# A dense layer by Strassen on pairs of token tiles, with the layer norm folded into its neighbours

## Chip, cores and metric

One NeuronCore of a Trainium2 chip runs the whole program. The metric is the device time of one execution in microseconds; lower is better. Times are medians of several executions; a profile is one execution.

## What is computed

Three stages follow each other on 2304 tokens of width 512. First, attention in chunks of 64 tokens. Second, a mixture of 8 experts, each with a hidden layer of 1024, weighted by eight rounds of row and column scaling. Third, the stage that the change touches (cut from the reference):

```
h = x @ w_in                                   # 2304x512 @ 512x1024
e = exp(h - max(h)); sm = e / (sum(e) + 1e-9)
solu = h * sm
ln = (solu - mean(solu)) / sqrt(var(solu) + 1e-6) * g_ln
return ln @ w_out                              # 2304x1024 @ 1024x512
```

w_in and w_out arrive as 64-bit floats and are turned into 32-bit ones on the chip.

## The kernel before

The program is unrolled, and every engine runs its instructions in the order in which they are written. Each 32-bit operand of a matmul is a pair of parts: `split` (L149) makes the high part on ScalarE (ACT) and the rest by a subtraction on VectorE (DVE) or GpSimd (POOL). A product takes three passes over these parts (PASSES3, L41).

**The experts.** They run as 96 units (3 passes over tokens, 32 weight blocks each) in the loop at L1203. One unit has seven slots; in each, `l1` (L738) issues one Strassen product of the first expert layer (six matmuls of 384 columns, L653) and `l2s` (L833) one half of a product of the second layer of two units earlier (six matmuls, L847). Weights come from DRAM by `w_load` (L617) on the SP queue. DVE adds the banks of `l1` and accumulates `l2s` into `acc`; POOL makes the sums and low parts of the hidden layer for `l2s` (`h_less` L679, `h_put` L665).

**Preparation of w_in and w_out.** From unit 35 on, one step of a list `prep` runs in slots 1, 3 and 5 of each unit (L1255). There are 16 chunks of 128x512, eight of each matrix, with ten steps each: a load (L907), seven steps of bit work on DVE (`mlp_steps`, L912), w_out rows scaled by g_ln on ACT (L949), `parts` (a split with POOL) and two stores of the parts (L957).

**The seam.** In unit 95 the parts of w_in are loaded (`load_in`, eight loads of 512 KB, tag `six`). Then 14 halves of `l2s` remain, numbered k = 0 to 13. They take PSUM banks from a ring of four (tag `r`) and each waits for DVE to have emptied the bank of four halves before. After k = 7, `mlp_b(0)` is issued; after k = 13 the loads of w_out's parts (`load_out`) and the tail begin.

**The tail.** For each of 18 token tiles: `mlp_a` splits x (ACT, DVE); `mlp_b` issues 24 matmuls of 512 columns into two PSUM banks (L1005), then the row maximum on DVE (L1019) and the exponential on ACT (L1020); `mlp_n` multiplies (L1025), takes statistics (L1026 to L1037, one power on POOL) and normalises on DVE (L1038); `mlp_c` transposes 128x1024 on TensorE (PE) in eight steps (L1050) and splits the result (ACT, DVE); `mlp_d` issues 24 matmuls (L1062), an eviction on ACT (L1072) and the store. The loop at L1296 issues b(s), c(s-1), n(s), d(s-2). The seven last sums of the experts' result (`l2s_sums`, L870) run on DVE between tiles 2 and 9, one for each tile.

Of the kernel before, what the change touches and what calls it, by code (L numbers as in the profile page):

```python
# [9 lines left out]
F32 = mybir.dt.float32  # L10
F32R = mybir.dt.float32r
# [33 lines left out]
def chunk_attention_sinkhorn_moe_solu_kernel(  # L45
# [74 lines left out]
    def six(shape, dt, name):  # L120
        return work.tile(shape, dt, tag="six", bufs=15, name=name)
# [7 lines left out]
    def two(shape, dt, name):  # L129
        return work.tile(shape, dt, tag="two", bufs=14, name=name)  # L130
# [762 lines left out]

    kept = {}
    for i in range(2):
        for s_ in range(2):
            kept[i, s_] = dram.tile([P, 4096], F32, name=f"kept{i}_{s_}")

    raw64 = {}

    def load_mlp(n):
        i, j = divmod(n, 8)
        src, r0, c0 = (w_in, (j // 2) * P, (j % 2) * 512) if i == 0 else (w_out, j * P, 0)
        raw64[n] = four([P, 512, 2], U32, f"wd{n}")
        nc.sync.dma_start(  # L907
            out=raw64[n].rearrange("p f w -> p (f w)"),
            in_=src.bitcast(U32)[r0:r0 + P, 2 * c0:2 * c0 + 1024],
        )  # L910

    def mlp_steps(n):  # L912
        i, j = divmod(n, 8)
        s = {}
        ts, stt = nc.vector.tensor_scalar, nc.vector.scalar_tensor_tensor


        def one():
            s["lo"], s["hi"] = raw64[n][:, :, 0], raw64[n][:, :, 1]
            s["b"] = two([P, 512], U32, f"wb{n}")  # L920
# [30 lines left out]
        def parts():  # L951
            s["p"] = [two([P, 512], F32R, f"wp{n}_{s_}") for s_ in range(2)]
            split(*s["p"], s["b"].bitcast(F32), nc.gpsimd)

        def store():
            for s_ in range(2):
                nc.sync.dma_start(  # L957
                    out=kept[i, s_][:, j * 512:(j + 1) * 512], in_=s["p"][s_].bitcast(F32)
                )

        return [one, two_, three, round_, rounded, size, flush_, parts, store]

    m_in, m_out = {}, {}

    def load_in(kk, s_):
        t = six([P, F], F32R, f"mi{kk}_{s_}")
        nc.sync.dma_start(out=t.bitcast(F32), in_=kept[0, s_][:, kk * F:(kk + 1) * F])
        m_in[kk, s_] = t

    def load_out(n0, n1):  # L970
        for n in range(n0, n1):
            f, s_ = divmod(n, 2)
            if n % 3 == 0:
                m_out["t"] = six([P, 3, DM], F32R, f"mo{n}")
            t = m_out["t"]
            nc.sync.dma_start(
                out=t[:, n % 3].bitcast(F32), in_=kept[1, s_][:, f * DM:(f + 1) * DM]
            )
            m_out[f, s_] = t[:, n % 3]

# [10 lines left out]
        )  # L991
        xa[t] = x

    def mlp_a(t):
        x = xa.pop(t)
        xm[t] = [wtile([P, KD, P], F32R, f"xm{t}_{i}") for i in range(2)]
        split(xm[t][0], xm[t][1], x)

    def mlp_b(t):
        x = xm.pop(t)  # L1000
        ph = bank2(f"mh{t}")
        for n in range(2):
            for kk in range(KD):
                for i, (a, c) in enumerate(PASSES3):
                    nc.tensor.matmul(  # L1005
                        ph[:, n * 512:(n + 1) * 512],
                        x[a][:, kk, :],
                        m_in[kk, c][:, n * 512:(n + 1) * 512],
                        start=(kk == 0 and i == 0),
                        stop=(kk == KD - 1 and i == 2),  # L1010
                    )
# [6 lines left out]
        r2 = small.tile([P, 1], F32, tag="r2", name=f"r2{t}")  # L1018
        nc.vector.tensor_reduce(out=nm, in_=ph, axis=AX.X, op=ALU.max, negate=True)  # L1019
        nc.scalar.activation(out=ex, in_=ph, func=AF.Exp, bias=nm, scale=1.0, accum_out=su)  # L1020
        stage[t] = (ph, ex, un, su, st, mv, r2)

    def mlp_n(t):
        ph, ex, un, su, st, mv, r2 = stage.pop(t)
        nc.vector.tensor_tensor(out=un, in0=ph, in1=ex, op=ALU.mult)  # L1025
# [12 lines left out]
        nc.vector.tensor_scalar(  # L1038
            out=un, in0=un, scalar1=mv[:, 0:1], scalar2=r2, op0=ALU.subtract, op1=ALU.mult
        )  # L1040
        ln[t] = un

    def mlp_c(t):
        un = ln.pop(t)
# [11 lines left out]
    def mlp_d(t, f0=0, f1=KF):  # L1056
# [12 lines left out]
        if f1 < KF:  # L1069
            return  # L1070
        ob = two([P, DM], F32, f"ob{t}")
        nc.scalar.activation(out=ob, in_=po.pop(t), func=AF.Copy)  # L1072
        nc.sync.dma_start(out=out[t * P:(t + 1) * P, :], in_=ob)


    with tc.manual_schedule():
# [91 lines left out]
        def x_steps(p, eng):  # L1168
# [34 lines left out]
        for n in range(NM):  # L1203
# [30 lines left out]
            if n == NM - 1:  # L1234
                for t in range(3):
                    mlp_x(t)
            apart = n < 4
            parts = [(j, d, i) for d in (0, 2) for j in range(2) for i in range(2)]
            for i in range(7):
# [7 lines left out]
                    elif i < 5:  # L1247
                        x_load(p + 1, XOPS[2 + i], nc.scalar)
                if n == NM - 1:
                    load_in(*divmod(i, 2))  # L1250
                if n != NU - 1 or i > 2:
                    run_w(2 if i < 4 or n == 0 else 1)
                if n:
                    run_side(1)
                if n > NU + 2 and i in (1, 3, 5) and prep:  # L1255
                    prep.popleft()()
                if NU > n > NQ and i in ((1, 2, 4, 6) if n in PLAIN else (2,)) and late:
                    late.popleft()()
# [82 lines left out]
```

## Time and profile before

| | us |
|---|---|
| median of 3 runs (1759.47 to 1763.54) | 1759.66 |
| the profiled execution | 1766.55 |
| its span, first to last instruction | 1764.7 |
| PE, DVE, ACT, POOL busy in the span | 1740.2, 1365.3, 626.6, 1093.5 |
| seam, first half of `l2s` after unit 95 | starts at 1530.64 |

Times in rows are microseconds from the start of the span, durations of one instruction in a group are in nanoseconds where a row says mean or gives min/median/max. PE counts as busy when a matmul is in its pipeline; ends of matmuls are modelled, so the distance between starts is the safer measure.

### The profile page before, as it was taken

How to read it: one execution, taken by the hardware profiler on the slowest of the kernel's cores; microseconds unless marked ns; L12 is line 12 of the kernel's file. 1: busy time of each engine (PE TensorE's matmuls, PEld its weight loads, DVE VectorE, ACT ScalarE, POOL GpSimd, SP SyncE). 2: the span in 40 equal slices, each digit the busy share in tenths (PEclk: the TensorE clock that was granted, in tenths of full speed). 3: DMA queues.
4: the chain of work that ended last, by engine and by line, in shares of the span. 5: the costliest groups of instructions: out<-in, count | busy, mean ns of one | idle time of the engine just before them, and what ended most of it. 6: DMA issues, size and time to landing. Idle time of an engine off the chain costs nothing. (4 is left out here: it accounts for less than half of the span.)

```text
span 1764.7 us, 32057 instructions
## 1 busy us (share of the span) xinstructions
PE 1740.2 (99%) x10809; PEld 1685.7 (96%) x10809; DVE 1365.3 (77%) x2249; ACT 626.6 (36%) x1424; POOL 1093.5 (62%) x1203
## 2 busy tenths in 40 slices
PE   8999999999999999999999999999999999999999
PEld 7899999999999999999999999999999999988887
DVE  6768888888987778787777688878787877776664
ACT  6743444444444233333332222232322222222222
POOL 2877988888887277778777756666656565400000
PEclk9999999999999999999999999999999999999999
DMA  9677899899899999989989999888888888931210
GB/s 220 181 247 257 296 325 335 311 343 326 319 324 330 348 331 339 336 297 351 310 296 340 341 328 369 301 284 283 282 263 276 281 275 255 314 108 45 66 49 30
DMA packets 299203, 481.45 MB, mean 273 GB/s; under 512 B 47248, under 2 KB 99616, under 8 KB 299040
## 3 DMA queue, kind: packets, MB, share of 16 engines
q1 hardware_dynamic: 298320, 475.47, 79.1%
q10 hardware_dynamic: 720, 3.93, 0.5%
q8 instruction: 87, 1.43, 0.3%
q14 instruction: 76, 0.62, 0.1%
HBM read 332.94 MB, written 146.35 MB: 272 GB/s over the span
## 5 line engine op out<-in xcount | busy, mean ns | idle before, releaser
L673 POOL TENSOR_TENSOR ho_T<-hT,ho_T 128x384 fp32r<-128x384 f32 x252 | 275.3, 1094 | 195.8 <-ACT ho_T L672 179.3
L796 PE MATMUL y<-h,w_A 128*128 128x384 f32 x1536 | 303.8, 335 | 0.5 <-DVE acc L823 0.5
L796 PEld LDWEIGHTS y<-h,w_A 128*128 128x128 f32 x1536 | 269.2, 188 | 1.3 <-ACT w_S L599 1.1
L672 ACT ACTIVATE ho_B<-hp 128x384 fp32r<-128x384 f32 x192 | 101.0, 526 | 418.6 <-DVE hp L706 410.4
L847 PE MATMUL y<-ho_T,wl_S 128*128 128x384 f32 x1152 | 231.4, 336 | 2.0 <-DMA wl_S<-wk 1.9
L152 POOL TENSOR_TENSOR w_A<-raw,w_A 128x256 fp32r<-128x256 f32 x224 | 173.2, 786 | 81.9 <-ACT w_A L151 77.5
L867 DVE TENSOR_TENSOR acc<-y,acc 128x768 f32<-128x768 f32 (+1 forms) x217 | 199.9, 923 | 24.5 <-PE y L847 24.3
L751 DVE TENSOR_TENSOR t<-Y,s 128x384 f32<-128x384 f32 x192 | 106.2, 553 | 136.5 <-PE Y L653 94.2
L847 PEld LDWEIGHTS y<-ho_T,wl_S 128*128 128x128 f32 x1152 | 203.1, 188 | 3.4 <-issue 2.2
L681 POOL TENSOR_TENSOR hT<-hp,hp 128x384 f32<-128x384 f32 x126 | 133.2, 1079 | 99.7 <-DVE hp L706 89.8
L672 ACT ACTIVATE ho_T<-hT 128x384 fp32r<-128x384 f32 x256 | 131.6, 516 | 124.6 <-POOL hT L681 119.9
L653 PE MATMUL Y<-x_T,wl_S 128*128 128x384 f32 x768 | 154.1, 335 | 0.4 <-DVE t L751 0.3
L653 PE MATMUL X<-x_B,wl_A 128*128 128x384 f32 x768 | 154.3, 335 | 0.0
L847 PE MATMUL y<-ho_B,wl_A 128*128 128x384 f32 x768 | 153.7, 334 | 0.5 <-DVE acc L867 0.4
L673 DVE TENSOR_TENSOR ho_B<-hp,ho_B 128x384 fp32r<-128x384 f32 x192 | 145.7, 759 | 3.9 <-ACT ho_B L672 3.3
L681 POOL TENSOR_TENSOR hT<-hp,hT 128x384 f32<-128x384 f32 x126 | 143.8, 1142 | 0.0
L1036 POOL TENSOR_TENSOR r<-r,mhalf 128x1 f32<-128x1 f32 x18 | 9.9, 550 | 208.5 <-DVE r L1033 208.5
L847 PEld LDWEIGHTS y<-ho_B,wl_A 128*128 128x128 f32 x768 | 134.7, 188 | 1.6 <-DVE acc L867 0.7
L653 PEld LDWEIGHTS Y<-x_T,wl_S 128*128 128x128 f32 x768 | 135.1, 188 | 1.1 <-DVE t L751 1.1
L653 PEld LDWEIGHTS X<-x_B,wl_A 128*128 128x128 f32 x768 | 135.4, 188 | 0.0
L823 DVE TENSOR_TENSOR acc<-y,acc 128x768 f32<-128x768 f32 (+1 forms) x132 | 118.9, 901 | 5.3 <-PE y L796 4.1
L152 POOL TENSOR_TENSOR w_S<-ws,w_S 128x256 fp32r<-128x256 f32 x128 | 103.0, 823 | 6.1 <-ACT w_S L151 6.1
(169 smaller groups left out, 3452.9 us busy)
## 6 DMA issues: line engine op xcount, KB each, us to landing
wl_S<-wk SPq DMA_DIRECT2D x512, 256.0 KB, 4.9
wl_A<-wk SPq DMA_DIRECT2D x384, 256.0 KB, 4.7
wk<-w_S SPq DMA_DIRECT2D x256, 256.0 KB, 3.6
wk<-w_A SPq DMA_DIRECT2D x192, 256.0 KB, 3.4
raw<-in_moe_w_dram SPq DMA_DIRECT2D x71, 512.0 KB, 5.8
sh<-spread SPq DMA_DIRECT2D x64, 192.0 KB, 5.4
kept<-wp SPq DMA_DIRECT2D x32, 256.0 KB, 4.2
xk_T<-x_T SPq DMA_DIRECT2D x8, 768.0 KB, 4.3
```

Of the source, the lines that this page charges most:

```text
L152: (eng or nc.vector).tensor_tensor(out=lo, in0=src, in1=hi.bitcast(F32), op=ALU.subtract)
L653: nc.tensor.matmul(b, w[:, a, kk, :], x[:, c, kk, :], start=(first and kk == 0 and n == 0), stop=(kk == 1 and n == 2), skip_group_check=no ...
L672: nc.scalar.activation(out=hi, in_=x, func=AF.Copy)
L673: f = lambda: eng.tensor_tensor(out=lo, in0=x, in1=hi.bitcast(F32), op=ALU.subtract)
L681: eng.tensor_tensor(out=hb[m, n], in0=hb[m, a], in1=hb[m, b], op=ALU.subtract)
L751: nc.vector.tensor_tensor(out=c_of[n], in0=bank_, in1=c_of[other], op=ALU.add)
L796: nc.tensor.matmul(y, wo2[u, f"A{d // 2 + 1}{f + 1}"][:, a, i * P:(i + 1) * P], h[:, c, f, :], start=(f == 0 and n == 0), stop=(f == 1 and ...
L823: nc.vector.tensor_tensor(out=at, in0=y, in1=at, op=ALU.add)
L847: nc.tensor.matmul(y, wo2[unit(m + q_)[1], wn][:, a, i * P:(i + 1) * P], hop[m // 2, bn][:, q_, c, :], start=(q_ == 0 and o == 0), stop=(q ...
L867: nc.vector.tensor_tensor(out=at, in0=y, in1=at, op=ALU.add)
L1036: nc.gpsimd.tensor_tensor(out=r2, in0=r2, in1=mhalf, op=ALU.pow)
```

## The change

The first dense layer takes two token tiles at once (a pair r is tiles 2r and 2r+1) and replaces eight block products by seven of six matmuls each, with sums of x blocks on POOL before and five additions of PSUM banks on DVE after. The operands of w_in (B11, T1, B22, T3, T2, B21, T4) are formed once in `prep`. w_out, scaled by g_ln, is stored whole, its mean over the rows is taken by a matmul with a constant matrix and subtracted, and the parts are stored; so the tail needs no subtraction of the mean. The factor of the norm is applied in ACT's last eviction, and `un` is transposed as it is. `prep` now has 203 steps: 98 for w_in, 72 for w_out, 33 for the mean; when 64 are left it runs in slots 0 to 5 of each unit. `load_in` reads 28 blocks of 128x512 in 12 loads (the first three into tag `V`). The diff, cut to its core:

```
     def mlp_steps(n):
...
+        def put_g():
+            nc.sync.dma_start(out=kept_g[:, j * 512:(j + 1) * 512], in_=s["b"].bitcast(F32))
...
+        def less(to, a, b):
...
+            nc.gpsimd.tensor_tensor(op=ALU.subtract, **x)
...
+    def mean_steps():
+        def load(j, new):
+            s[j] = new([P, 512], F32, f"wg{j}")
+            nc.sync.dma_start(out=s[j], in_=kept_g[:, j * 512:(j + 1) * 512])
+        def add(j):
+            nc.gpsimd.tensor_tensor(out=s[0], in0=s[0], in1=s.pop(j), op=ALU.add)
+        def mean():
+            nc.gpsimd.memset(ratio, 1.0 / F)
+            pm = bank("wmean")
+            nc.tensor.matmul(pm, ratio, s.pop(0), start=True, stop=True)
+            s["m"] = vtile([P, 512], F32, "wmean")
+            nc.scalar.activation(out=s["m"], in_=pm, func=AF.Copy)
+        def less(j):
+            nc.gpsimd.tensor_tensor(out=s[j], in0=s[j], in1=s["m"], op=ALU.subtract)
...
+        r = [lambda: (load(0, vtile), load(1, two))]
+        for j in range(1, 8):
+            r.append(lambda j=j: (load(j + 1, two) if j < 7 else None, add(j)))
+        r.append(lambda: (mean(), load(0, two)))
+        for j in range(8):
+            r.append(lambda j=j: (load(j + 1, two) if j < 7 else None, less(j)))
+            r.append(lambda j=j: parts(j))
+            r.append(lambda j=j: store(j))
...
+    def mlp_s(r):
+        x0, x1 = xa[2 * r], xa[2 * r + 1]
+        ts = nc.gpsimd.tensor_tensor
+        s = xsum[r] = [two([P, 2, 2, P], F32, f"xs{r}_{i}") for i in range(2)]
+        ts(out=s[0][:, 0], in0=x1[:, 0:2], in1=x1[:, 2:4], op=ALU.add)
...
+    def mlp_a(r):
...
+        a = put("A1", x0.rearrange("p (h k) x -> p h k x", h=2))
+        b = put("S12", s[0])
+        d = put("S34", s[1])
+        xm[r, "A22"] = put("A22", x1[:, 2:4])
...
+    def mlp_b(r, i):
...
+        for kk in range(2):
+            for n, (a, c) in enumerate(PASSES3):
+                nc.tensor.matmul(b, x[a][:, kk, :], m_in[xn, c, kk],
...
+        if i == 0:
+            mb["s1"] = two([P, 512], F32, f"ms{r}")
+            nc.scalar.activation(out=mb["s1"], in_=b, func=AF.Copy)
+        for to, x, other in {
+            1: (("t0", b, "s1"),), 3: (("t1", b, "s1"), (r1[:, 512:], at["Z"], "t1")),
+            5: ((b, b, "s1"),), 6: ((b, b, "t0"),),
+        }.get(i, ()):
...
+            nc.vector.tensor_tensor(out=to, in0=x, in1=mb[other], op=ALU.add)
+        if i == 5:
+            mlp_e(2 * r + 1, r1)
+        elif i == 6:
+            mlp_e(2 * r, r0)
...
     def mlp_n(t):
...
-        nc.vector.tensor_tensor(out=r2, in0=r2, in1=su, op=ALU.mult)
-        nc.vector.tensor_scalar(
-            out=un, in0=un, scalar1=mv[:, 0:1], scalar2=r2, op0=ALU.subtract, op1=ALU.mult
-        )
+        nc.gpsimd.tensor_tensor(out=r2, in0=r2, in1=su, op=ALU.mult)
...
-        nc.scalar.activation(out=ob, in_=po.pop(t), func=AF.Copy)
+        nc.scalar.activation(out=ob, in_=po.pop(t), func=AF.Copy, scale=r2s.pop(t))
...
-                if n > NU + 2 and i in (1, 3, 5) and prep:
+                if n > NU + 2 and (i in (1, 3, 5) or len(prep) <= fast and i != 6) and prep:
...
+        order = (0, 1, 4, 3, 2, 5, 6)
...
             if k == 7:
-                mlp_b(0)
-                mlp_a(2)
+                for i in order:
+                    if i == 5:
+                        mlp_a(1)
+                    mlp_b(0, i)
+                mlp_m(1)
+                mlp_m(0)
...
+        mlp_c(1)
+        mlp_c(0)
+        mlp_n(1)
         mlp_n(0)
...
+        for r in range(1, NR):
+            t1, t0 = 2 * r + 1, 2 * r
+            if r + 1 < NR:
+                mlp_s(r + 1)
+            for i in order:
+                mlp_b(r, i)
+            mlp_m(t1)
+            mlp_m(t0)
+            if r + 1 < NR:
+                mlp_a(r + 1)
+            mlp_d(t1 - 2)
+            mlp_c(t1)
+            mlp_n(t1)
+            for _ in range(2):
+                if sums:
+                    sums.popleft()()
...
+            mlp_n(t0)
+            mlp_d(t0 - 2)
+            mlp_c(t0)
         mlp_d(NT - 1)
+        mlp_d(NT - 2)
```

`mlp_e` is the row maximum and the exponential, `mlp_m` the multiplication. After the seam the order is l2s k = 0 to 7, b(0), m(1), m(0), l2s k = 8 to 13, then c(1), c(0), n(1), n(0) and the loop. Unit 95 now also holds `mlp_s(0)` (slot 3) and `mlp_a(0)` (slot 5), and k = 6 `mlp_s(1)`.

## Rows read from the trace of the kernel before

**Rows 1.** The page's first part: engines of the whole span.

```profile
PE 1740.2 (99%) x10809; PEld 1685.7 (96%) x10809; DVE 1365.3 (77%) x2249; ACT 626.6 (36%) x1424; POOL 1093.5 (62%) x1203
```

**Rows 2.** The chain of waits in the tail: start us, us, what.

```profile
1590.59 5.49 PE po L1062 x24
1596.08 5.44 PE mh L1005 x24
1601.52 0.87 PE lt L1050 x8
```

**Rows 3.** Timeline of the seam: start us, us, engine, line, operation [idle before].

```profile
1530.64 4.33 PE L847 MATMUL y<-ho_B,wl_A 128*128 128x384 f32 x24
...
1532.07 1.94 DVE L152 TENSOR_TENSOR xm<-xa,xm 128x512 fp32r<-128x512 f32 x2
...
1540.49 5.64 PE L1005 MATMUL mh<-mi,xm 128*128 128x512 f32 x24
...
1549.80 2.52 DVE L867 TENSOR_TENSOR acc<-y,acc 128x384 f32<-128x384 f32 x5
1550.41 2.04 PEld L847 LDWEIGHTS y<-ho_T,wl_A 128*128 128x128 f32 x12 [0.40 <-DVE acc L867]
...
1554.40 0.14 DVE L1026 TENSOR_SCALAR su<-su 128x1 f32<-128x1 f32 x1
...
1556.41 0.21 DVE L1033 TENSOR_SCALAR r<-mv,r 128x1 f32<-128x1 f32 x1
...
1565.96 1.06 PE L1050 MATMUL lt<-ident,un 128*128 128x128 f32 x8 [0.98 <-DVE un L1038]
```

**Rows 4.** Groups of the stretch 1560 to 1765: count, then busy us, mean ns.

```profile
L152 DVE TENSOR_TENSOR lnt<-lt,lnt 128x512 fp32r<-128x512 f32 x36 | 23.2, 686 | 31.3 <-ACT lnt L151 31.3
...
L1025 DVE TENSOR_TENSOR un<-mh,ex 128x1024 f32<-128x1024 f32 x17 | 20.7, 1216 | 1.3 <-ACT ex L1020 1.3
L1019 DVE TENSOR_REDUCE nm<-mh 128x1 f32<-128x1024 f32 x16 | 19.6, 1225 | 21.9 <-PE mh L1005 21.9
...
L875 DVE TENSOR_TENSOR acc<-acc,acc 128x768 f32<-128x768 f32 x7 | 6.7, 953 | 0.0
```

**Rows 5.** Instructions of L152, L397 and L673: ns min/median/max, first and last start.

```profile
L152 POOL TENSOR_TENSOR wp<-wb,wp x16: 1275/1298/1477, 674.0 to 1414.4; 128x512 fp32r<-128x512 f32 x16
...
L397 PE MATMUL pc<-pw,ratio x16: 307/308/413, 108.1 to 141.4; 128*128 128x171 f32 x16
...
L673 DVE TENSOR_TENSOR ho_B<-hp,ho_B x192: 541/559/1425, 599.3 to 1530.3; 128x384 fp32r<-128x384 f32 x192
```

**Rows 6.** Timelines of POOL, SP and PE in unit 87.

```profile
1402.48 1.99 POOL L681 TENSOR_TENSOR hT<-hp,hp 128x384 f32<-128x384 f32 x2 [3.10 <-DVE hp L706]
1404.42 1.19 POOL L673 TENSOR_TENSOR ho_T<-hT,ho_T 128x384 fp32r<-128x384 f32 x1
...
1405.51 0.32 SPq L621 DMA_DIRECT2D wl_S<-wk  x1
...
1410.00 1.20 PE L653 MATMUL Y<-x_T,wl_A 128*128 128x384 f32 x6
```

**Rows 7.** DMA issues: queue, count, KB each, median us to landing.

```profile
mo<-kept SPq DMA_DIRECT2D x16, 256.0 KB, 5.2
```

**Rows 8.** Timeline of PE after a late load, and one window (PEclk before DMA).

```profile
984.38 1.39 PE L847 MATMUL y<-ho_T,wl_S 128*128 128x384 f32 x6 [1.68 <-DMA wl_S<-wk]
...
987.22 2.12 PE L847 MATMUL y<-ho_T,wl_S 128*128 128x384 f32 x6
...
990.31 1.21 PE L847 MATMUL y<-ho_T,wl_S 128*128 128x384 f32 x6
...
986.00:988.00 2.00, 2.00 (x8) 2.00 (x7) 0.00 (x0) 0.49 (x2) 2.00 (x3) 0.50 0.99 336
```

**Rows 9.** Windows, seam and unit 83: PE, PEld, DVE, ACT, POOL; PEclk, DMA share, GB/s.

```profile
1535.00:1540.00 5.00, 4.37 (x22) 3.73 (x23) 5.00 (x11) 1.55 (x4) 0.00 (x0) 1.00 1.07 381
...
1340.54:1355.10 14.56, 14.56 (x86) 14.56 (x85) 13.55 (x22) 3.33 (x7) 6.98 (x7) 1.00 0.83 260
```

More of the change, by code (lines that the diff above doesn't have):

```diff
@@ L891, in chunk_attention_sinkhorn_moe_solu_kernel, with mlp_chunk @@
     }
[L896 to L899, printed above, removed]
+    kept_in = dram.tile([P, 28 * 512], F32, name="kept_in")
+    kept_out = [dram.tile([P, 4096], F32, name=f"kept_out{s_}") for s_ in range(2)]
+    kept_g = dram.tile([P, 4096], F32, name="kept_g")
+    M_IN = ("B11", "B12", "B22", "B21")
     raw64 = {}
+    def mlp_chunk(n):
+        i, j = divmod(n, 8)
+        if i == 0:
+            c, name = divmod(j, 4)
+            name = M_IN[name]
+            j = 2 * (2 * (int(name[1]) - 1) + c) + int(name[2]) - 1
+            return i, j, c, name
+        return i, j, 0, None
     def load_mlp(n):
-        i, j = divmod(n, 8)
+        i, j, _, _ = mlp_chunk(n)
         src, r0, c0 = (w_in, (j // 2) * P, (j % 2) * 512) if i == 0 else (w_out, j * P, 0)
@@ L955, in store @@
-        def store():
+            split(*s["p"], f, nc.gpsimd)
+        def store(n_=None):
             for s_ in range(2):
+                k = 4 * XOPS.index(n_) + 2 * s_ + c
+                to = kept_in[:, k * 512:(k + 1) * 512]
+                nc.sync.dma_start(out=to, in_=s["p"][s_].bitcast(F32))
+        def less(to, a, b):
+            f = s["b"].bitcast(F32)
+            x = {"out": f, "in0": f, "in1": f}
+            for k, v in (("in0", a), ("in1", b)):
+                if v != name:
+                    x[k] = x["out"] = carried[v]
+            nc.gpsimd.tensor_tensor(op=ALU.subtract, **x)
+            carried[to] = x["out"]
@@ new lines, in mlp_steps, with keep_b @@
+        steps = [one, two_, three, round_, rounded, size, flush_]
+        if i == 1:
+            return steps + [put_g]
+        def keep_b():
+            carried[name] = s["b"].bitcast(F32)
+        put = lambda v: [lambda: parts(v), lambda: store(v)]
+        if name == "B11":
+            return steps[:-1] + [lambda: (flush_(), keep_b())] + put("B11")
+        if name == "B12":
+            return steps[:-1] + [
+                lambda: (flush_(), keep_b()), lambda: less("T1", "B12", "B11")
+            ] + put("T1")
@@ new lines, in mlp_steps, with parts, store @@
+        if name == "B22":
+            return steps + put("B22") + [
+                lambda: (less("T3", "B22", "B12"), less("T2", "B22", "T1"))
+            ] + put("T3") + put("T2")
+        return steps + put("B21") + [lambda: less("T4", "B21", "T2")] + put("T4")
+    def mean_steps():
+        s = {}
+        def load(j, new):
+            s[j] = new([P, 512], F32, f"wg{j}")
+            nc.sync.dma_start(out=s[j], in_=kept_g[:, j * 512:(j + 1) * 512])
+        def add(j):
+            x = s.pop(j)
+            nc.gpsimd.tensor_tensor(out=s[0], in0=s[0], in1=x, op=ALU.add)
+        def mean():
[6 more added lines that the diff above has]
+            nc.gpsimd.tensor_tensor(out=s[j], in0=s[j], in1=s["m"], op=ALU.subtract)
+        def parts(j):
+            s["p", j] = [two([P, 512], F32R, f"wp{8 + j}_{s_}") for s_ in range(2)]
+            split(*s["p", j], s.pop(j), nc.gpsimd)
+        def store(j):
+            for s_, p in enumerate(s.pop(("p", j))):
@@ L957, in store @@
                 nc.sync.dma_start(
-                    out=kept[i, s_][:, j * 512:(j + 1) * 512], in_=s["p"][s_].bitcast(F32)
+                    out=kept_out[s_][:, j * 512:(j + 1) * 512], in_=p.bitcast(F32)
                 )
-        return [one, two_, three, round_, rounded, size, flush_, parts, store]
-    m_in, m_out = {}, {}
[L965 to L968, printed above, removed]
+        r = [lambda: (load(0, vtile), load(1, two))]
@@ new lines, in mean_steps, with load_in @@
+        for j in range(1, 8):
[5 more added lines that the diff above has]
+            r.append(lambda j=j: store(j))
+        return r
+    m_in, m_out = {}, {}
+    def load_in(n):
+        if n < 3:
+            t = vtile([P, 1, 512], F32R, f"mi{n}")
+            k0, k1 = n, n + 1
+        else:
+            t = six([P, 3, 512], F32R, f"mi{n}")
+            k0, k1 = 3 * n - 6, min(3 * n - 3, 28)
+        nc.sync.dma_start(
+            out=t[:, :k1 - k0].bitcast(F32).rearrange("p k x -> p (k x)"),
+            in_=kept_in[:, k0 * 512:k1 * 512],
+        )
+        for k in range(k0, k1):
+            x, r = divmod(k, 4)
+            m_in[XOPS[x], r // 2, r % 2] = t[:, k - k0]
@@ L992, in mlp_x @@
         xa[t] = x
[L994 to L1010, printed above, removed]
-                    )
+    xsum = {}
@@ new lines, in chunk_attention_sinkhorn_moe_solu_kernel @@
+    mb = {}
+    def mlp_b(r, i):
+        if i == 0:
+            mb["r0"], mb["r1"] = bank2(f"mh{r}_0"), bank2(f"mh{r}_1")
+        r0, r1 = mb["r0"], mb["r1"]
+        at = {"X": r0[:, :512], "Z": r0[:, 512:], "Y": r1[:, :512]}
+        wn, xn, bn = PRODUCTS[i]
+        b, first = at[bn], i in (0, 1, 4)
+        x = xm.pop((r, wn))
+        for kk in range(2):
+            for n, (a, c) in enumerate(PASSES3):
+                nc.tensor.matmul(
+                    b, x[a][:, kk, :], m_in[xn, c, kk],
+                    start=(first and kk == 0 and n == 0),
+                    stop=(kk == 1 and n == 2),
+                    skip_group_check=not first,
+                )
+        if i == 0:
+            mb["s1"] = two([P, 512], F32, f"ms{r}")
[4 more added lines that the diff above has]
+        }.get(i, ()):
+            if isinstance(to, str):
+                mb[to] = two([P, 512], F32, f"m{to}{r}")
+                to = mb[to]
+            nc.vector.tensor_tensor(out=to, in0=x, in1=mb[other], op=ALU.add)
[3 more added lines that the diff above has]
+            mlp_e(2 * r, r0)
@@ L1179, in chunk_attention_sinkhorn_moe_solu_kernel @@
         )
+        fast = 64
+        prep.extend(mean_steps())
         events = {}
@@ L1234, in chunk_attention_sinkhorn_moe_solu_kernel @@
             if n == NM - 1:
+                assert not prep, len(prep)
                 for t in range(3):
+                    load_in(t)
+            if n == NM - 2:
+                for t in range(2):
                     mlp_x(t)
```

98 lines of the change are left out of this document (62 added, 36 removed).

## The prediction

> **What bounds the kernel now.** I read the engines' totals first: PE is busy for 1740.2 of 1764.7 us [rows 1], so a change pays only where it takes work or a wait off PE. The chain of waits in the tail shows the same from inside: it runs over PE alone, 24 matmuls of a first dense layer 5.44 us, eight transposes 0.87, 24 matmuls of the second 5.49, again and again [rows 2]. Then the timeline of the seam, where the order of work changes: between unit 95 and the tail PE waits for DVE three times, 1.5 us over the first eight halves (9.85 us from the first to the first dense matmul, against eight times 1.04), 0.4 before k = 12 and 1.0 before the first transposes of tile 1 [rows 3]. Last I read what runs beside PE where the new steps will lie.
>
> The profiled execution took 1766.55 us, 1.85 more than its span and 6.9 more than the median, 1759.66. I sum differences against the profiled execution and put them on the median.
>
> **Strassen's saving.** A pair of tiles takes 7 x 6 = 42 matmuls instead of 48. Nine pairs save 54, at 5.44 / 24 = 0.227 us each [rows 2]: **-12.2**. A pair then holds PE for 42 x 0.227 + 2 x (0.87 + 5.47) = 22.2 us. The Trainium skill ("TensorE: Matmul & The Clock Gate", Back-to-back issue gap) gives some 131 ns for one of 512 columns in a sustained stream; by that the 54 would be worth 7.1 us, an estimate, and the time would be 5.1 us later. The trace disagrees with it, at 227 ns.
>
> **What the tail's other engines get.** Per pair POOL takes four sums of 128x256 and four low parts, each at most 1.3 [rows 5], under 11 us of 22.2, in place of two powers; ACT takes one copy and four high parts for two. Both lie beside PE, whose operands are ready half a pair ahead. DVE loses two low parts of x and two normalisations and gains five additions of 128x512 with one operand in PSUM, like the low parts of the transposes at 0.69 [rows 4]: about 15.5 us a pair before and after. The totals fit; what counts is when DVE reaches the addition t0, for product S3 (the fourth issued) overwrites the bank that t0 reads. Scaling the output rides on an eviction that exists: nothing, covered by ACT's slack. After the last matmul nothing changes.
>
> **The seam.** Two low parts of x leave DVE there (1.94 for both) [rows 3], so of the 1.5 us before the first dense layer I keep 0.3: **-1.2**. Call T the end of the pair's last product. DVE then has: addition 0.69 and maximum 1.23 from T - 1.2, addition, maximum, two multiplications of 1.22 [rows 4], done at T + 5.3 with gaps. Only then it empties the bank of k = 8 (0.5) [rows 3], while PE reaches k = 12 at T + 4.2: a wait of 1.7 in place of 0.4, **+1.3**. DVE goes on with five more banks, four low parts, and two rows of statistics of 2.2 each (1554.40 to 1556.62 without the power) [rows 3], until T + 16.4, and t0 ends at T + 17.05. PE starts pair 1 at T + 6 x 1.04 + 1.7 + 2 x 0.87 = T + 9.7 and wants product S3 after three products of 1.36, at T + 13.8: a wait of 3.2. The wait of 1.0 for the normalisation goes: **+2.2**. Behind the waiting matmul the whole tail is queued.
>
> **Inside the pairs.** From the end of a pair's products DVE does its 5.3, waits for the first transposes to about 7.5, then two low parts (to 9.0), statistics (11.2), two of the seven sums at 0.95 [rows 4] (13.1), statistics (15.3), low parts (16.7), t0 (17.35). PE wants S3 at 2 x 6.34 + 4.08 = 16.8. Pairs 1 to 3 carry two sums: 0.65 each, **+2.0**; without sums there are 1.3 us in hand.
>
> **Preparation.** 203 steps instead of 160 end in unit 91 instead of 88: 138 at three a unit to unit 80, then six. POOL gets more splits in units 35 to 66, DVE fewer steps a unit: nothing, covered by the seven slots for which each step's result waits. In units 81 to 86 DVE gets 4.7 steps a unit instead of 2.1; a unit with 22 DVE instructions, as those will have, was busy for 13.55 of 14.56 and cost PE nothing [rows 9]: nothing; if that cover is gone, up to 1 us a unit. Stores and loads grow by 36 of 256 KB; SP waits behind steps that are now one slot apart, which the weights' lead of five slots (10.4 us) against a landing of 5.2 [rows 7] covers.
>
> **The mean's matmul** is new on PE, in slot 5 of unit 87, and PE takes it in order. Before it POOL must add eight blocks, one a slot from unit 86, between its own work. POOL's two differences of unit 87 end at 1404.5 [rows 6]; a DVE step of the preparation that delayed them is gone, so I take 1403.6. From there: four adds of 1.3 [rows 5], two low parts and two differences of about 1.05 [rows 6], one fill of 0.2: 9.5, so 1413.1. The last load is issued behind the weights at 1405.5 and lands after 5.2, about 1411 [rows 6, 7]: in time. PE arrives at 1410.0 + 1.04 [rows 6]: a wait of **+2.1**. Bounds: nothing, if POOL runs ahead; 8.2, if the last add waits for one more landing on top of 3.0. I take the value of the rows. The matmul itself is in full 32 bits: those of L397 are two records of 0.31 for 171 columns [rows 5], of which some 0.2 is pipeline (5.64 against 5.44 for 24) [rows 2, 3]; so 0.7 to 1.85 for 512 columns; **+0.8**, near the lower end because records overlap.
>
> **The clock.** After an idle stretch of 1.68 PE ran at 0.50 of the granted clock, 1.2 of 2.4 GHz, and four groups of six took 5.93 instead of 4.16: 1.8 lost [rows 8]. So the waits of 2.1 and 3.2 should each lose 1.8: **+3.5** (none to three times that as bounds). A lower clock after the wait at k = 12 would come off the next wait, which DVE sets.
>
> Sum: -12.2 - 1.2 + 1.3 + 2.2 + 2.0 + 2.1 + 0.8 + 3.5 = **-1.5**: 1758.2 us. No change that a measurement can tell, which takes 0.3%, 5.3 us.
>
> **Rivals.** *The new waits are shorter and the clock holds (faster).* POOL reaches the last add before PE, and DVE's chain is a microsecond shorter. For it: the rows price POOL's operations while DVE competes; against it: both chains are sums of measured durations in a fixed order. Without the two slow stretches and the wait at the mean: -1.5 - 3.5 - 2.1 = -7.1, 1752.6; with the waits inside the pairs gone too, 1750.6.
>
> *The seam becomes bound by transfers (slower).* w_in comes in 28 blocks of 0.262 MB instead of eight loads of 0.524: 3.1 MB more, and the queue is full there, share 1.07 at 381 GB/s [rows 9]. From 1515 the new loads, 15 weights and two x tiles are 11.0 MB, 28.9 us, so they land by 1544; the last product of b(0) wants them at about 1547.5. It decides from 4 us of lateness on; if all the extra shows, 8.3 us, it is 1766.5.
>
> *POOL holds up DVE's sums (slower).* Subtractions with both operands in SBUF took from 0.54 to 1.43 on DVE [rows 5]. If each of six sums is held for one operation of POOL, 1.3, pairs 1 to 3 wait 2.6 longer each: +7.8, 1766.0. Against it: POOL has finished its parts at about 9.6 of the pair, before the sums at 11.2. The Trainium skill ("SBUF — State Buffer", Who interferes with whom) says that a DVE instruction with two SBUF inputs and a GpSimd one that reads SBUF exclude each other, and one with a single SBUF input does not. The spread agrees; by the rule t0 and the statistics are safe.
>
> That the products would not run at 0.227 has no weight: groups of six into changing banks keep 1.04 [rows 3].
>
> **Chances.** The sum as it stands 0.48, all of it within 0.3%. Shorter waits 0.31, faster. Transfers 0.14 and held sums 0.07, slower: 0.21. The range goes from the rival's 1750.6 to the transfers' 1766.5, and leaves out a tenth on either side.
>
> **What would show it.** Pairs of 22.2 us in the chain; a wait of PE at k = 12 near 1.7; one at the fourth product of pair 1 near 3.2, ended by DVE's t0; one at the mean's matmul near 2.1, ended by POOL; a granted clock of 0.50 behind the last two. Wrong: no wait at the mean, a clock of 1.00 throughout, PE waiting for the loads of w_in, or for t0 in pairs without sums.

## The result, and the profile after

| | before | after |
|---|---|---|
| time, us (median; lowest to highest) | 1761.6 (1759.47 to 1763.63) | 1782.76 (1782.11 to 1783.74) |
| ratio, 95% interval | | 1.0114 (1.0102 to 1.0126) |
| profiled execution, span, us | 1766.55, 1764.7 | 1783.35, 1781.6 |
| mean granted clock | 0.998 | 0.994 |

The change made the kernel slower by 1.1%, some 20 us. The forecast was 1.5 us less than before, and the range ended at 1766.5.

The page's totals and, below them, the answer on who kept PE waiting (total us, times, longest), both of the kernel after:

```profile
PE 1735.7 (97%) x10757; PEld 1679.4 (94%) x10757; DVE 1373.6 (77%) x2240; ACT 644.6 (36%) x1458; POOL 1208.8 (68%) x1323
```

```profile
PE mh L1145 <- DVE mh L1161: 13.7, 9, 1.6
PE y L847 <- DMA wl_S<-wk: 3.6, 2, 2.3
PE wmean L1025 <- POOL ratio L1023: 3.2, 1, 3.2
PE mh L1145 <- DVE mt L1161: 2.7, 1, 2.7
...
PE y L847 <- DVE acc L867: 1.4, 1, 1.4
```

PE has 52 instructions less than in [rows 1] and is busy for 4.5 us less, but the span is 16.9 longer: the time went into waits and into stretches at a lower clock. The largest wait, nine times 1.5 us, stands in no step of the prediction. The chain of the tail, the work that PE had to get through one after the other, shows one pair's products (start, us, what):

```profile
1598.65 5.47 PE mh L1145 x24
...
1604.14 0.70 DVE mt L1161
...
1604.87 0.71 DVE mh L1161
...
1605.62 4.40 PE mh L1145 x18
1610.02 5.45 PE po L1220 x24
```

In [rows 2] this chain ran over PE alone. Now it leaves PE in every pair, after four products (24 matmuls), for two additions of DVE: t1, and c22 = Z + t1. The timeline of PE gives the period, from the first second dense layer of one pair to that of the next:

```profile
1605.62 3.04 PE L1145 MATMUL mh<-mi,xm_A 128*128 128x512 f32 x12 [1.52 <-DVE mh L1161]
...
1609.86 5.61 PE L1220 MATMUL po<-mo,lnt 128*128 128x512 f32 x24
...
1633.93 2.43 PE L1220 MATMUL po<-mo,lnt 128*128 128x512 f32 x10
```

It is 24.07 us, against 23.58 for two tiles before (second dense layers at 1602.15 and 1625.73) and 22.2 forecast. What answers to [rows 3], the seam, and to the unit of [rows 6], again as PE's timeline:

```profile
1408.88 1.20 PE L653 MATMUL Y<-x_T,wl_A 128*128 128x384 f32 x6
1413.27 2.07 PE L1025 MATMUL wmean<-wg,ratio 128*128 128x512 f32 x2 [3.19 <-POOL ratio L1023]
1414.36 2.59 PE L847 MATMUL y<-ho_T,wl_A 128*128 128x384 f32 x6
...
1535.37 4.33 PE L847 MATMUL y<-ho_B,wl_A 128*128 128x384 f32 x24
1541.99 3.72 PE L847 MATMUL y<-ho_B,wl_S 128*128 128x384 f32 x12 [2.29 <-DMA wl_S<-wk]
...
1547.93 1.55 PE L1145 MATMUL mh<-mi,xm_A 128*128 128x512 f32 x6
...
1565.11 2.36 PE L847 MATMUL y<-ho_T,wl_A 128*128 128x384 f32 x12 [1.39 <-DVE acc L867]
...
1576.05 2.25 PE L1145 MATMUL mh<-mi,xm_S 128*128 128x512 f32 x6 [2.71 <-DVE mt L1161]
```

From the first half to the first dense product it is 12.56 us (before: 9.85), with a wait for weights in the middle. The other three waits are the forecast ones: the mean, half 12, and t0 of pair 1. Windows behind three of the four: the mean, the weights, and t0 of pair 1 with the wait of 1.52 that follows it (columns as in [rows 9]; PEclk stands before the DMA share):

```profile
1414.00:1416.00 2.00, 2.00 (x5) 1.20 (x4) 0.00 (x0) 0.62 (x2) 0.00 (x0) 0.50 0.05 17
...
1542.00:1546.00 4.00, 4.00 (x14) 3.86 (x15) 4.00 (x9) 1.05 (x2) 1.26 (x2) 0.59 1.11 366
...
1580.00:1582.00 2.00, 2.00 (x5) 1.61 (x6) 0.00 (x0) 0.00 (x0) 0.00 (x0) 0.50 0.00 0
```

PE is busy throughout in each, at a granted clock of 0.50 to 0.59, and does half the work or little more.

### The profile page after: what moved, and what is told of

It is laid out like the page before. It is cut to its first block, busy times and chain, and to the rows that moved or that the text cites. A ratio compares the mean times of both kernels' runs of the same rounds, so it can differ in the third digit from the quotient of the medians.

```text
span 1781.6 us, 32257 instructions
## 1 busy us (share of the span) xinstructions
PE 1735.7 (97%) x10757; PEld 1679.4 (94%) x10757; DVE 1373.6 (77%) x2240; ACT 644.6 (36%) x1458; POOL 1208.8 (68%) x1323
## 4 chain that ended last, share of the span: by engine, by line
PE 83%; DMA 5%; DVE 5%; POOL 3%; ACT 2%; issue 2%; SPq 0%; DVEq 0%; ACTq 0%; POOLq 0%
PE y L847 22%; PE Y L653 15%; PE y L796 14%; PE Z L653 10%; PE X L653 10%; PE po L1220 6%; PE mh L1145 5%; DMA wl_A<-wk 3%; DMA wl_S<-wk 1%; POOL ho_T L673 1%; PE lt L1208 1%; POOL hT L681 1%; DMA wg<-kept_g 1%; ACT qt L204 1%; DVE kt L206 0%
## 5 line engine op out<-in xcount | busy, mean ns | idle before, releaser
L673 POOL TENSOR_TENSOR ho_T<-hT,ho_T 128x384 fp32r<-128x384 f32 x252 | 279.1, 1109 | 176.7 <-ACT ho_T L672 154.4
L152 POOL TENSOR_TENSOR w_A<-raw,w_A 128x256 fp32r<-128x256 f32 x224 | 173.2, 786 | 81.8 <-ACT w_A L151 74.2
L673 DVE TENSOR_TENSOR ho_B<-hp,ho_B 128x384 fp32r<-128x384 f32 x192 | 146.4, 763 | 3.8 <-ACT ho_B L672 3.1
L152 POOL TENSOR_TENSOR w_S<-ws,w_S 128x256 fp32r<-128x256 f32 x128 | 102.9, 821 | 6.1 <-ACT w_S L151 6.1
L706 DVE SCALAR_TENSOR_TENSOR hp<-X,sh 128x384 f32<-128x384 f32 x128 | 71.2, 556 | 40.4 <-PE X L653 19.6
```

The costliest lines, as they stand in the source:

```text
L152: (eng or nc.vector).tensor_tensor(out=lo, in0=src, in1=hi.bitcast(F32), op=ALU.subtract)
L673: f = lambda: eng.tensor_tensor(out=lo, in0=x, in1=hi.bitcast(F32), op=ALU.subtract)
```

## The experiments

Times are compared through the ratio to the kernel before, run in turn with it on the same chip; 0.001 is 1.76 us. All edits are on the changed kernel (1.0114) unless said. A difference between two rows is known to some 3 us, so a small one is read from the time between two fixed points of the traces. In the code, `...` stands for lines that are left out.

| kernel | us | ratio, 95% interval | against the change, us |
|---|---|---|---|
| z_own | 1769.62 | 1.0040 (1.0025 to 1.0055) | -13.0 |
| late_c22 | 1774.72 | 1.0073 (1.0055 to 1.0091) | -7.2 |
| n_late | 1777.43 | 1.0085 (1.0069 to 1.0102) | -5.1 |
| mean_gap | 1777.85 | 1.0089 (1.0070 to 1.0108) | -4.4 |
| seam_dma | 1781.88 | 1.0105 (1.0091 to 1.0119) | -1.6 |
| parts_early | 1781.91 | 1.0112 (1.0088 to 1.0137) | -0.4 |
| seam_both | 1780.79 | 1.0098 (1.0081 to 1.0116) | -2.8 |
| centre_only | 1767.71 | 1.0024 (1.0015 to 1.0033) | -15.9 |
| all | 1760.47 | 0.9989 (0.9980 to 0.9998) | -22.0 |
| all2 | 1758.88 | 0.9979 (0.9971 to 0.9988) | -23.8 |
| all3 | 1757.03 | 0.9970 (0.9955 to 0.9984) | -25.4 |
| all4 | 1751.88 | 0.9950 (0.9936 to 0.9964) | -28.9 |

**The wait inside the pairs: z_own.** The fifth product writes bank X; c22 reads bank Z. In the change both are halves of one tile, r0.

```
+ mb["Z"] = bank(f"mz{r}")
  ...
- at = {..., "Z": r0[:, 512:], ...}
+ at = {..., "Z": mb["Z"], ...}
  ...
- 6: ((b, b, "t0"),)
+ 6: ((r0[:, 512:], b, "t0"),)
```

> Bank Z gets a tile of its own (four-bank ring) instead of the second half of the tile whose first half is bank X; the same 42 matmuls and the same additions, c22 and c12 now written from Z into the halves of the two-bank tiles. Theory (the wait of 1.5 us at the fifth product of each pair comes of order being kept by tile: it writes X and waits for c22, which only reads Z): the wait at the fifth product goes; at most 0.2 us is left at the sixth, which writes the tile into which c22 is written. Pair period 24.06 -> 22.2 to 22.5, nine pairs, so 14 to 16.5 us: 1766 to 1769. Rival (DVE is simply late there, with t1 and c22 behind other work, and holds whatever product comes next): PE still waits 1.3 to 1.6 us in each pair, and the time stays within 3 us of 1782.8.

Measured: -13.0 us. Timelines of PE and DVE in z_own:

```profile
1596.87 1.52 PE L1146 MATMUL mh<-mi,xm_S 128*128 128x512 f32 x6
1598.23 1.52 PE L1146 MATMUL mh<-mi,xm_A 128*128 128x512 f32 x6
1599.15 0.70 DVE L1162 TENSOR_TENSOR mh<-mz,mt 128x512 f32<-128x512 f32 x1
...
1599.91 1.67 PE L1146 MATMUL mh<-mi,xm_A 128*128 128x512 f32 x6 [0.16 <-DVE mh L1162]
...
1602.80 5.61 PE L1221 MATMUL po<-mo,lnt 128*128 128x512 f32 x24
```

The fifth product starts 1.36 behind the fourth, and c22 (1599.15) runs beside it. The sixth writes bank Y, the other half of the tile into which c22 is written, and still waits, 0.16. The period is 22.68 (1580.12 to 1602.80). It was expected at 22.2 to 22.5, and the time ends just above the expected 1766 to 1769: the small wait costs more than it shows (below).

**The same wait from the other side: late_c22.** The tiles stay; c22 is emitted behind the fifth product.

```
- 3: (("t1", b, "s1"), (r1[:, 512:], at["Z"], "t1")),
+ 3: (("t1", b, "s1"),), 2: ((r1[:, 512:], at["Z"], "t1"),),
```

> Tiles as in the changed kernel; only the addition c22 is emitted behind the fifth product (into X) instead of ahead of it. If order is kept by tile: the fifth product no longer waits, c22 can start only when that product has ended (it shares the tile that c22 reads), and the sixth product, which writes the tile that c22 writes, waits 0.8 to 1.0 us; 0.5 to 0.7 a pair is won: 1776 to 1779. If order is kept by bank: c22 runs during the fifth product as it may start after t1, the sixth waits at most 0.2, and 12 to 16 us are won: 1767 to 1771. If DVE is simply late: no change, 1781 to 1784.

Measured: -7.2 us, a little more than the expected 1776 to 1779 (the four executions spread from 1772.19 to 1779.39). Timelines of PE and DVE in one pair:

```profile
1597.89 1.52 PE L1145 MATMUL mh<-mi,xm_A 128*128 128x512 f32 x6
...
1598.10 0.69 DVE L1161 TENSOR_TENSOR mt<-mh,ms 128x512 f32<-128x512 f32 x1 [1.88 <-PE mh L1145]
1599.45 0.70 DVE L1161 TENSOR_TENSOR mh<-mh,mt 128x512 f32<-128x512 f32 x1 [0.67 <-PE mh L1145]
...
1600.21 1.66 PE L1145 MATMUL mh<-mi,xm_A 128*128 128x512 f32 x6 [0.79 <-DVE mh L1161]
```

The fifth product no longer waits. DVE, free after t1, sits idle 0.67 us until that product has ended before it may read Z, though the product wrote X. Then the sixth waits 0.79. So order is kept by tile, not by bank, and DVE was not late. The banks did not need it: in z_own c22 reads Z while the fifth product writes X. The Trainium skill ("PSUM — Partial Sum Buffer", Summary: rules for kernel authors) has a reader that runs beside a matmul use a different bank and guards by bank; the runs agree, since X and Z are different banks, and with separate tiles the wait goes.

**t0 of pair 1: n_late.** The statistics of tiles 1 and 0 move behind t0, t1 and c22 of pair 1 (four buffers instead of three for their small tiles).

```
- mlp_n(1); mlp_n(0)
  ...
      mlp_b(r, i)
+     if r == 1 and i == 3: mlp_n(1)
  mlp_m(t1)
+ if r == 1: mlp_n(0)
```

> The statistics of tiles 1 and 0 (4.4 us of DVE ahead of t0 of pair 1) are emitted inside pair 1, behind t0, t1 and c22, and nothing else moves. Theory (t0 is 2.7 us late because these statistics stand ahead of it, and the low clock behind the wait follows from the idle stretch): the wait of 2.71 goes, and with it the stretch at 0.50 of the clock, together 4.5 to 6 us, of which 0.5 to 2 comes back as a wait for the first transposes of pair 1 or for t0 of pair 2: 1777 to 1780. Rival (other work of the seam, the emptied banks of k = 8 to 13 and the four low parts, makes t0 late): the wait shrinks by less than 1 us, and the time stays within 1.5 us of 1782.8.

Measured: -5.1 us. Products 2 to 4 of pair 1 in PE's timeline:

```profile
1569.65 4.24 PE L1145 MATMUL mh<-mi,xm_S 128*128 128x512 f32 x18
```

The wait of 2.71 is gone, the products run on until the fifth (1.52, as in every pair), and the clock between 1574 and 1586 is 1.00. No wait for the transposes of pair 1 came in its place; at t0 of pair 2 some 0.3 did (products 2 to 4 take 4.59 us there, 4.24 in the change).

**The mean: mean_gap.**

```
- nc.gpsimd.memset(ratio, 1.0 / F)   (in mean)
+ r.append(lambda: nc.gpsimd.memset(ratio, 1.0 / F))
+ r += [lambda: None] * 3
  r.append(lambda: (mean(), load(0, two)))
  ...
- fast = 64
+ fast = 68
```

> In the preparation three empty steps stand between the last of the seven adds for the mean (the fill of the matrix of 1/1024 is emitted with it) and the step that issues the mean's matmul and its load. Theory (PE takes the matmul in order and reaches it 3.2 us before POOL has made its operands): the wait of 3.19 and the low clock behind it go, 4.5 to 5.5 us: 1777 to 1778.5. Rival (POOL is so far behind in these units that three slots do not help): the wait is still over 2 us three slots later, and the time is within 1.5 us of 1782.8. Second rival: the wait goes but the low clock stays, being set by something else in that stretch: about 3 us are won.

Measured: -4.4 us in the ratio; the four executions spread from 1774.89 to 1781.69, so the size is known less well than the mechanism. Timeline of PE:

```profile
1422.05 1.20 PE L653 MATMUL Y<-x_T,wl_S 128*128 128x384 f32 x6
1423.09 1.02 PE L1024 MATMUL wmean<-wg,ratio 128*128 128x512 f32 x2
1423.55 1.61 PE L847 MATMUL y<-ho_B,wl_A 128*128 128x384 f32 x6
```

No wait is left, the granted clock stays at 1.00, and between its neighbours the full 32-bit matmul takes 0.46 us (1423.09 to 1423.55) and draws out the next group.

**The seam: seam_dma, parts_early, seam_both.** Two suspects: w_in's blocks ahead of the weights in SP's queue (the wl_S that PE waited for was issued at 1532.82 and came 9.04 us later), and POOL's low parts of x beside DVE.

```
(seam_dma)    if n == NM - 1:
-                 load_in(3 + i)
+                 if i < 5: load_in(3 + i)
  ...
-             if k in (2, 5): load_in(10 + k // 3)
-             if k == 1: mlp_x(2); mlp_x(3)
+             if k in (1, 2, 4, 5): load_in({1: 8, 2: 9, 4: 10, 5: 11}[k])
+             if k == 5: mlp_x(2); mlp_x(3)
(parts_early)     if i == 3:
                      mlp_s(0)
+                     mlp_a(0)
-                 if i == 5:
-                     mlp_a(0)
(seam_both)   both
```

> Order of loads at the seam alone: blocks 8 and 9 of w_in are issued after halves 1 and 2 of the last second-layer group (10 and 11 after halves 4 and 5), the two x tiles of pair 1 after half 5, so that the weights of that group stand ahead of them in SP's queue. Theory (PE waits 2.29 us for wl_S because 1.5 MB of w_in stand ahead of it in a full queue, and the clock falls behind that wait): the wait falls below 0.7 and the time by 2.5 to 4.5 us: 1778 to 1780. Rival (there are simply too many bytes between 1515 and 1548 us, share 1.02 to 1.16): the lateness reappears at another load, the products of the first pair wait for mi or for their x, and the time stays within 1.5 us of 1782.8.

> The parts of x for the first pair (four high parts on ACT, four low parts on POOL) are emitted two slots earlier in unit 95, right behind its sums; loads as in the changed kernel. Theory (POOL's low parts stand beside DVE's four differences hT, with both operands in SBUF, and stretch them from 0.54 to 1.3 to 1.6 us each, but PE waits for the weights in the same place anyway): the four differences take 2.0 to 2.6 us instead of 4.5, DVE is no longer late, and PE still waits 1.5 to 2.3 us for wl_S: 1781 to 1783. Rival (DVE's lateness is what counts): the wait of 2.29 falls below 1 us, 1778 to 1780.

> The loads reordered (0.9 won alone, as PE then waited for DVE's emptied banks) and the parts of x two slots earlier, on the changed kernel. Theory (two causes for one loss of 2.3 us and the low clock behind it; each hides the other): together the waits between the halves fall below 0.8 us in all and the clock holds, from the first half to the first dense product 9.0 to 10.2 us instead of 12.6: 1778 to 1780. Rival (a third cause, the bytes in flight or POOL's last two low parts beside DVE): still 11 us or more, 1781 to 1783.

Measured: -1.6, -0.4 and -2.8 us. The intervals of all three overlap that of the change, so these times alone do not tell them apart. The time from the first half to the first dense product does, one profiled execution for each kernel (8.32 us without a wait, 9.85 in the kernel before):

| loads | parts of x | kernels | us |
|---|---|---|---|
| as in the change | as in the change | after, z_own, late_c22, n_late, mean_gap | 12.56, 11.33, 11.35, 12.16, 11.86 |
| reordered | as in the change | seam_dma, all, all2 (below) | 12.21, 12.75, 13.22 |
| as in the change | two slots earlier | parts_early | 9.85 |
| reordered | two slots earlier | seam_both, all3, all4 (below) | 9.76, 9.80, 9.80 |

The loads reordered win nothing by themselves: in seam_dma PE waited for DVE's emptied banks instead (0.67 and 0.97) and the clock fell behind that, which neither its theory nor its rival had. The parts two slots earlier bring the seam back to the time of the kernel before, and the reordering adds no more than 0.1. PE's timeline in parts_early:

```profile
1539.49 4.32 PE L847 MATMUL y<-ho_B,wl_A 128*128 128x384 f32 x24
1544.96 2.44 PE L847 MATMUL y<-ho_B,wl_S 128*128 128x384 f32 x12 [1.15 <-DMA wl_S<-wk]
...
1549.34 1.55 PE L1145 MATMUL mh<-mi,xm_A 128*128 128x512 f32 x6
```

The wait for wl_S was 1.15, between the 1.5 to 2.3 of the theory and the less than 1 of the rival, and the granted clock stayed at 1.00; DVE's four differences took 2.58 us, as expected (2.0 to 2.6). Chance has a part in it: this execution's wl_S landed 5.33 us behind the first half, against 5.89 to 7.36 in the five of the first row, and its first load of w_in in unit 95, which the edit does not touch, was already 0.65 us or more ahead of theirs. With the landing of the change, 6.49, four halves (4.16) would still have followed: some 10.7 us, an estimate. So DVE's lateness is shown as a cause; what the order of the loads is worth beside it stays open.

The time of parts_early hides the gain: in its profiled execution the seam begins 4.1 us later than in the change (1539.49 against 1535.37), and 3.1 of these were lost in the first 620 us. Why DVE was late shows in the timelines of DVE and POOL, first of the kernel after, then of seam_both:

```profile
1536.68 2.85 POOL L152 TENSOR_TENSOR xm_S<-xs,xm_S 128x512 fp32r<-128x512 f32 x2
...
1536.81 3.13 DVE L681 TENSOR_TENSOR hT<-hp,hp 128x384 f32<-128x384 f32 x2
...
1540.87 1.34 DVE L681 TENSOR_TENSOR hT<-hp,hT 128x384 f32<-128x384 f32 x1
```

```profile
1537.92 1.47 DVE L681 TENSOR_TENSOR hT<-hp,hp 128x384 f32<-128x384 f32 x2
...
1540.26 0.54 DVE L681 TENSOR_TENSOR hT<-hp,hT 128x384 f32<-128x384 f32 x1
```

Beside POOL's parts two differences take 3.13 us on DVE. One more takes 1.34 instead of 0.54, beside the low parts of the hidden layer, which POOL makes later now (from 1540.49). With both edits it is 9.76 us from the first half (1535.15) to the first product (1544.91). The ratio's 2.8 us is what the seam had lost, but is known to some 3 us only; the expected 1778 to 1780 was missed by 0.8, inside the interval.

**The other half of the change alone: centre_only**, on the kernel before: w_out's blocks stored unsplit, mean and centring as in the change, the two normalising steps of DVE gone, the factor at the eviction; first dense layer and order of the tail as before.

```
- return [one, ..., flush_, parts, store]
+ return steps + ([put_g] if i == 1 else [parts, store])
+ prep.extend(mean_steps())
- nc.vector.tensor_scalar(out=un, ..., op0=ALU.subtract, op1=ALU.mult)
```

> The kernel before with only the centring part of the change: w_out kept unsplit, its mean by POOL's adds and one matmul, centred blocks stored, un transposed unnormalised, the factor applied at the last eviction; first dense layer, its loads and the order of the tail as before. Theory (the centring costs the wait at the mean, its matmul and the clock behind it, some 5 us, and gives back the wait of 1.0 before the first transposes): 1764 to 1768 against 1762.6. Rival (with 18 steps less in the preparation the mean's operands are ready when PE comes, or the tail gains from a DVE that is freed): 1760.5 to 1763.

Measured: 0.24% slower than before, 4.2 us. The mean falls into another unit here, and PE waits there for POOL:

```profile
1325.90 2.07 PE L985 MATMUL wmean<-wg,ratio 128*128 128x512 f32 x2 [3.79 <-POOL ratio L983]
```

The clock is 0.50 behind it. The waits of 0.21 and 0.98 before the first transposes are gone. The time lies in the expected 1764 to 1768. The remaining 0.9% of the change's loss comes with the Strassen half and its seam.

**Everything mended: all, all2, all3, all4.** all is z_own, n_late, mean_gap and seam_dma; all2 also moves the two multiplications for un; all3 adds parts_early; all4 gives bank Y its own tile too.

```
(all2)  -  mlp_m(1); mlp_m(0)      (behind b(0))
        +  if k == 9: mlp_m(1)
        +  if k == 11: mlp_m(0)
(all4)  +  mb["Y"] = bank(f"my{r}")
        -  5: ((b, b, "s1"),)
        +  5: ((r1[:, :512], b, "s1"),)
```

> Four edits together: Z in its own tile (13.1 us won alone), the statistics of tiles 1 and 0 inside pair 1 (5.3 alone), the three empty steps before the mean's matmul (4.9 alone), the loads of the seam reordered. Theory (four separate losses, each on PE's path): they add, less about 1 us that the tile edit and the statistics share at pair 1: 1754 to 1758 against 1762.6 of the kernel before, 0.3 to 0.5 % faster. Rival (one loss hides behind another, with DVE's t0 late in pairs 2 to 4 when pairs are 1.4 us shorter and the statistics later): t0 waits of 1 to 2 us in pairs 2 to 4, 1759 to 1763.

> As the kernel with four edits, and the two multiplications that make un for tiles 1 and 0 are emitted after halves 9 and 11 of the last group instead of ahead of half 8. Theory (the wait of 1.39 at half 12 comes of the bank of half 8 being emptied behind these multiplications): that wait goes, 1.2 to 1.4 us more: 1753 to 1757. Rival (un is then late for the first transposes): the same wait moves to the transposes, and the time is within 0.5 us of the kernel with four edits.

> All edits so far together, with the parts of x of the first pair two slots earlier. Theory (the waits of 1.26 and 1.24 us for DVE's emptied banks and the clock at 0.50 behind them are all that is left of the seam's loss): 2.5 of waits and 1.6 of clock go, 1754 to 1756.5 against 1758.9 without that edit and 1762.2 of the kernel before. Rival (the low parts only move beside other work of DVE, the additions and low parts of unit 95, which then run late): within 1 us of 1758.9.

> All edits so far, and bank Y in a tile of its own as well (c21 is written from it into the two-bank tile). In the kernel without this edit the start of the sixth product is 1.68 us behind that of the fifth, and of the seventh 1.49 behind the sixth, where 1.36 is a product without a wait. Theory (the sixth product writes the tile into which c22 is written, and waits for it; with Y apart no product of a pair waits for an addition but the fourth, for t0): both fall to 1.36 to 1.40, a pair is 0.40 to 0.47 us shorter, nine pairs 3.6 to 4.2: 0.9943 to 0.9952 of the kernel before, some 1753. Rival (that the change of bank behind DVE's work costs 0.3 whatever the tiles are, or that the ring of four single banks, now with eight tiles a pair, makes transposes or second dense layers wait): no gain or a loss, 0.997 or more.

all fell short (1760.5 where 1754 to 1758 was expected): with the loads reordered and the parts of x where the change has them, DVE's emptied banks held PE at the seam by 1.26 and 1.24. all2 (1753 to 1757) and all3 (1754 to 1756.5) ended above their ranges too, by 1.9 and 0.5; all4 came as expected. Against the version ahead of it, all2 won 1.8 (half 12 no longer waits), all3 1.6 (the seam takes 9.80 instead of 13.22, clock 1.00), all4 3.5 (a pair takes 22.24 instead of 22.7). By the intervals none of these steps is clear of the noise; what each took away is read from the traces. The timeline of PE in all4:

```profile
1582.88 1.65 PE L1147 MATMUL my<-mi,xm_S 128*128 128x512 f32 x6 [0.79 <-DVE mt L1163]
...
1588.45 5.61 PE L1222 MATMUL po<-mo,lnt 128*128 128x512 f32 x24
...
1606.61 1.52 PE L1147 MATMUL mh<-mi,xm_A 128*128 128x512 f32 x6
1607.97 1.52 PE L1147 MATMUL my<-mi,xm_A 128*128 128x512 f32 x6
1609.33 1.52 PE L1147 MATMUL mz<-mi,xm_S 128*128 128x512 f32 x6
1610.69 5.61 PE L1222 MATMUL po<-mo,lnt 128*128 128x512 f32 x24
```

A pair is 22.24 us, and its last products follow each other at 1.36. Only pair 2 takes longer, 23.30: its fourth product waits 0.79 for t0 (1582.88), which DVE reaches late now that pair 1 also holds the statistics of tiles 1 and 0. all4 is faster than both kernels: 0.5% under the kernel before (0.9936 to 0.9964), 1.6% under the change.

## Why the prediction was wrong

**The step that failed is "Inside the pairs"**, which rests on the sentence "what counts is when DVE reaches the addition t0" under "What the tail's other engines get". DVE's five additions were priced as a total over a pair, and only t0 was asked which product waits for it. The addition c22 was not asked, and its wait stood at nothing without a reason given: it reads Z and the next product writes X, but the kernel makes both of one tile (the line `at` in the edit of z_own). The wait is 1.52, and 1.83 in the period (24.07 against 22.24), nine times 16.5 us. Giving Z a tile took the period to 22.68, giving Y one to 22.24; the times, 13.0 and 3.5 us, agree with that as far as their intervals go. No rival held it, so the range could not.

**Strassen's saving** was right: a pair is 23.58 before and 22.24 in all4, nine times 1.34 is 12.1, against 12.2. Here the 227 ns of the trace held.

**The seam, -1.2, was 2.7 the other way** (12.56 against 9.85), a miss of 3.9; in the four other kernels whose seam is that of the change it was 1.5 to 2.3 the other way. The low parts did leave DVE, but POOL's work, put beside DVE's four differences, took more: 3.13 and 1.34 for three of them, at 0.54 each 1.62. The prediction looked for this exclusion in the tail, with the sums, where it did not happen (L875 took 0.95 at the median, as before). By the Trainium skill ("SBUF — State Buffer", Who interferes with whom) a DVE instruction with two SBUF inputs contends with a GpSimd one that reads SBUF; the rows at 1536 agree. The rival of the transfers was right in part: PE waited not for the last blocks of w_in at 1547.5, but 2.29 us for the weights of half 4, behind those blocks; reordering the loads alone won nothing.

**The mean** was right in kind: 3.19 against 2.1. That POOL was done at 1413.22, where 1413.1 was worked out, is luck: the kernel after stands 1.12 us ahead of the one before at this place (the group at 1410.00 in [rows 6] starts at 1408.88), and POOL's two differences as well (1401.31 against 1402.48, in POOL's timeline of the kernel after):

```profile
1401.31 1.99 POOL L681 TENSOR_TENSOR hT<-hp,hp 128x384 f32<-128x384 f32 x2
...
1413.02 0.20 POOL L1023 MEMSET ratio<- 128x128 f32 x1
```

So seen from PE they came no earlier than before, where the prediction took 0.9 off, and POOL was about a microsecond later than worked out. Matmul 1.1 against 0.8 (at half clock; 0.46 in mean_gap at 1.00), clock 1.4 against 1.8 (one group in 2.43 instead of 1.04).

**t0 of pair 1** (2.71 against 3.2) and **half 12** (1.39 against 1.7) were right to half a microsecond. **The clock** cost more than the 3.5: 1.4 at the mean; 1.8 at the seam, which is part of its miss above (the halves from 1541.99 to 1547.93 take 5.94 us, where four are 4.16); and 2.7 behind t0 (the products of pair 1 take 16.87, from 1568.97 to 1585.84, those of pair 2 11.46, and 2.71 is the wait). **The sums**, +2.0, cost nothing: t0 held up no pair behind sums, neither in the change nor in z_own with its shorter pairs. There t0 of pair 2 ended at 1596.57, 16.45 behind the end of pair 1's products, where 17.35 was added up (and 17.35 less 16.8 is 0.55, not the 0.65 that went into the sum). **The preparation** cost nothing, as forecast: in units 35 to 86 PE's waits sum to 6.4 us before and 6.2 after, and the low clock took 1.7 in both.

Sum of the misses: 16.5 (pairs) + 3.9 (seam) + 1.0 (mean: 5.7 against 4.7) + 0.4 (t0 and its clock: 5.4 against 5.0) - 0.3 (half 12) - 2.0 (sums) = 19.5. The profiled executions are 16.8 us apart and the ratio makes 20.1; against the -1.5 of the forecast that is 18.3 and 21.6, so the terms cover the miss to within some 2 us.

## What to carry to other kernels

When a buffer is made of several banks, ask of every operation which tile it touches, not which bank: in this program, two operations on different halves of a tile are put in order, at the price of everything that the first one waits for. A tile for each bank costs a few lines, and was here worth more than the arithmetic that the algorithm saved. Where work moves to another engine, look at what that engine's new work stands beside, and in a queue of loads at what it stands ahead of. An edit in one place is judged by the time between two fixed points around it: at the seam that showed which of two suspects counted, where the time of the whole run did not.

## What the runs showed of the hardware that was not expected

The granted clock does not follow from the length of the wait alone. PE's timeline of n_late and seam_dma, then a window of each:

```profile
1541.01 3.55 PE L847 MATMUL y<-ho_B,wl_S 128*128 128x384 f32 x12 [1.74 <-DMA wl_S<-wk]
```

```profile
1542.00:1546.00 4.00, 4.00 (x15) 3.75 (x14) 4.00 (x9) 0.87 (x2) 1.82 (x2) 0.57 1.07 377
```

```profile
1413.66 1.12 PE L1025 MATMUL wmean<-wg,ratio 128*128 128x512 f32 x2 [3.30 <-DMA wl_S<-wk]
```

```profile
1414.00:1416.00 2.00, 2.00 (x10) 1.57 (x9) 0.00 (x0) 1.01 (x2) 0.09 (x1) 1.00 0.05 18
```

After an idle stretch of 1.74 us the mean clock of four microseconds was 0.57; after one of 3.30, in another kernel, it stayed at 1.00 (2.4 GHz). A short wait also costs more than it shows: in z_own the sixth product waits 0.16, but from the fifth's start to the second dense layer it is 4.57 us, against 4.08 in all4.
